# DeltaNet and SwiGLU on one core: where chunk 2 makes the sums of the gate and value weights

## The chip, the cores and the metric

The kernel runs on one NeuronCore of a Trainium2 chip, in float32 throughout. The metric is the time of one execution on the device in microseconds (us). A core has five engines that run side by side, each through its own instructions in order: TensorE (PE in the profile; PEld is its loading of weights), VectorE (DVE), ScalarE (ACT), GpSimd (POOL) and SyncE (SP), which here only issues DMA transfers. Where one engine needs another's result it waits on a semaphore.

## The reference

Four sequences with eight heads of size 48 go through a delta-rule attention over 768 steps. Its output, laid side by side by head (3072 tokens of 384 numbers), goes through a SwiGLU block with 1536 hidden units.

```python
k_n = k / (norm(k) + 1e-6)
for t in range(S):
    y[t]  = q[t] @ state
    v_old = k_n[t] @ state
    state = state + beta[t] * outer(k_n[t], v[t] - v_old)
x = y.transpose(0, 2, 1, 3).reshape(B * S, H * D)
g = x @ w_gate
out = (g * sigmoid(g) * (x @ w_val)) @ w_out
```

## The kernel before

**Chunks.** The 768 steps are cut into 12 chunks of 64. For a chunk, attention turns K and Q, makes products of K with K and of Q with K (`gram`), inverts a triangular matrix for each head and two chunks (`invert`, with `substitute` as 31 steps of two VectorE operations), joins the halves of that inverse (`join_1`, `join`), and carries the state forward in four steps (`advance`): first p_r and p_y, the products of K and Q with the state, and the subtraction of p_r from V (L770); then p_u (L775), copied into `uu`; then p_s and p_y (L806, L794); then the transposes p_f and the copy into `x_ffn` (L843). The FFN of chunk c, 256 tokens, runs on TensorE while attention of chunk c + 1 is threaded through it.

**The FFN of chunk 2.** `FAST` is 3. Chunks 0 to 2 compute the FFN plainly, chunks 3 to 11 by a scheme of block sums which saves products (`gate_val_fast`, `output_fast`) and which needs sums of blocks of the weights. Chunk 2 is the last plain one (`c == FAST - 1`). Its loop (L1443) runs over six pairs of hidden blocks, f = 0, 2, 4, 6, 8, 10. `gate_val` (L1002) does for each pair: the gate product (12 matmul instructions at L1009), SiLU on ScalarE (L1018), the value product (12 more), the product of the two on VectorE (L1023, called h here), then `point`, the sums, and `fill`. The outputs of the chunk's two halves follow (`output`, L1036, with a copy at L1044 and two stores issued by ScalarE at L1053).

**What threads attention in.** `point(c + 1)` issues one piece of the next chunk's attention. In the six pairs of chunk 2 these are, in order: the second half of a join (L639); the transposes of K and Q (L424), behind each of which stand eight block loads of the next chunk into the buffer just read, issued by SP (L169); the gram products (L447) with the masking of one result on VectorE (L465); then the first three steps of `advance`. `fill(n)` spends about n units on the inverse (the steps of `substitute`, L519 and L525, the transposes of `turn`, L489, those at L687 and L692, and four ScalarE copies at L698) and stops in the middle where n runs out; the next `fill` goes on from there. So the order on each engine is fixed by the order of these calls. No scheduler changes it.

**The sums.** `sums_of_w(f)` (L880) does two things. For three of the pairs it makes one set r of three sums, each in two VectorE operations of 128x256 (L1080, L1077), and stores each to device memory as soon as it is ready, by SP (L894). The three sums have one buffer each, used for all three sets: `w_s[1]` is h_f_99, `w_s[2]` is h_f_100, and `w_s[4]` is half of p_sb_125. So the next set can't be written until the last one's stores have landed. The set r = 0 stays in the buffers for the first round of chunk 3; the others are loaded back later (L941). For f of 6 and more it also overwrites two blocks of the weights with a difference (two operations, L1077), so the sums that need such a block must have been made by then. In the kernel before, the sets are made at pairs 2, 4 and 6, in the order r = 1, 2, 0.

**What follows.** After both outputs, `join` of the next inverse begins (L716 on TensorE, L722 on ScalarE), and chunk 3's first fast round (L917) starts: a product p_x, copied by ScalarE to p_y (L945), a product p_w, and a product that accumulates on p_y (both from L928).

Of the kernel before, what the change touches and what calls it, by code (L numbers as in the profile page):

```python
# [20 lines left out]
def kernel(  # L21
# [57 lines left out]
    def ps_ffn(shape, name, bank=None):  # L79
        if bank is None:  # L80
            taken.append(name)
            bank = (len(taken) - 1) % 4
        n = 1
        for m in shape[1:]:
            n *= m
        p = ffn_banks[bank][:, 0:n]
        return p if len(shape) == 2 else p.rearrange("p (x n) -> p x n", x=shape[1])
# [225 lines left out]
    for b in range(2):  # L313
# [5 lines left out]
            fill=0.0,  # L319
# [536 lines left out]
    def new_h(c, f, at):  # L856
        hs[c, f] = hp[at].rearrange("p (i n) -> p i n", i=2)
# [17 lines left out]
    def w_pair(m, t, f):  # L875
        return (wg_sb, wv_sb)[m][:, t, 128 * f : 128 * f + 256].rearrange(
            "p (i n) -> p i n", i=2
        )

    def sums_of_w(f):  # L880

        if 2 <= f <= 6:
            r = f // 2 % 3
            f1, f2 = 2 * r, 2 * r + 6
            for n in (1, 2, 4):
                for m in range(2):
                    s_ = w_s[n][:, 2 * m : 2 * m + 2]
                    if n == 1:
                        plus(s_, w_pair(m, 0, f2), w_pair(m, 1, f2))
                    elif n == 2:  # L890
                        minus(s_, w_s[1][:, 2 * m : 2 * m + 2], w_pair(m, 0, f1))
                    else:
                        minus(s_, w_pair(m, 1, f1), w_s[2][:, 2 * m : 2 * m + 2])
                nc.sync.dma_start(out=kept[n, r], in_=w_s[n])  # L894
        if f >= 6:
            for m in range(2):
                minus(w_pair(m, 0, f), w_pair(m, 0, f - 6), w_pair(m, 0, f))
# [104 lines left out]
    def gate_val(c, f, fill, within=None, behind=None):  # L1002

        ps = {}
        for w_sb, name in ((wg_sb, "p_gate"), (wv_sb, "p_val")):
            ps[name] = ps_ffn([128, 2, TOK], name)
            for i in range(2):
                for t in range(KT):
                    nc.tensor.matmul(  # L1009
                        ps[name][:, i],  # L1010
                        w_sb[:, t, (f + i) * 128 : (f + i + 1) * 128],
                        xts[c][:, t],
                        start=(t == 0 and (i == 0 or c < 2)),
                        stop=(t == KT - 1),
                        skip_group_check=True,
                    )
            if name == "p_gate":
                nc.scalar.activation(sil, ps[name], ACTF.Silu)  # L1018
                fill(2)
                if within is not None:  # L1020
                    point(within)
        new_h(c, f, len(hs) if c < 2 else f // 2)
        nc.vector.tensor_tensor(out=hs[c, f], in0=sil, in1=ps["p_val"], op=ALU.mult)  # L1023
        if behind is not None:
            point(behind)
        if c == FAST - 1:
            sums_of_w(f)
        fill(3)

    def output(c, bp, fill, between=()):  # L1030
        p_o = ps_ffn([128, DM], "p_o", bp if c == FAST - 1 else None)
# [28 lines left out]
    FAST = 3  # L1060
# [15 lines left out]
    def minus(out, a, b):  # L1076
        nc.vector.tensor_tensor(out=out, in0=a, in1=b, op=ALU.subtract)  # L1077

    def plus(out, a, b):
        nc.vector.tensor_tensor(out=out, in0=a, in1=b, op=ALU.add)  # L1080
# [92 lines left out]
    def converts(n):  # L1173
        if todo:
            convert(todo[:n])
            del todo[:n]
# [36 lines left out]
    def fill_some(n):  # L1213
        while n > 0 and fills:
            did = next(fills[0][1], 0)
            if did == 0:
                inverted.add(fills.pop(0)[0])
            if did == WAIT:
                return
            n -= did or 1  # L1220
# [51 lines left out]
    def point(c):  # L1272

        mine = c < NCH and steps("advance", c) < 4 and may_advance(c)
        if mine and steps("advance", c) > 0:
            step("advance", advance, c)
        elif not prep_step(c - 1) and mine:
            step("advance", advance, c)
# [12 lines left out]
    def fill(n):  # L1291
        if todo:

            filled.append(n)
            converts(2 if len(filled) < 4 else 1)
            if len(filled) == 1:
                converts(1)
        else:
            after_weights()
            fill_some(n)  # L1300
# [3 lines left out]
    def after_weights():  # L1304
        if not done:
            done.append(1)
            nc.gpsimd.memset(ztp[1], 0.0)
            fills.insert(0, (1, second_inverse[0]))
# [6 lines left out]
    with tc.manual_schedule(  # L1315
# [101 lines left out]
        for c, f in pairs:  # L1417
            early = c == 0 and f < 8
            if c == 1 and f == 0:
                finish(1)  # L1420
            elif f > 0:
                point(1 if early else 2)
            need((6, 12, 18, 18, 24, 24)[f // 2])
            gate_val(c, f, fill, 1 if early else None)
# [11 lines left out]
        for c in range(2, NCH):  # L1436
            point(c + 1)
            if c >= FAST:
                for r in range(ROUNDS):
                    gate_val_fast(c, r, fill)  # L1440
                output_fast(c, fill)
            else:
                for f in range(0, FT, 2):  # L1443
                    gate_val(c, f, fill, behind=c + 1)
                output(c, 0, fill)
                point(c + 1)
                output(c, 1, fill)
            finish(c + 1)
            x_sums(c + 1)
# [30 lines left out]
```

## Time and profile before

| | us |
|---|---|
| runs of the kernel before (four) | 725.7, 726.38, 724.74, 723.41 |
| median | 725.22 |
| the profiled execution | 725.7 |
| its span, first to last instruction | 724.0 |
| TensorE busy in the span | 685.5 |
| VectorE busy | 464.4 |
| ScalarE busy | 255.0 |
| the gate and value products of chunk 2 (L1009) | 190.09 to 235.4 |
| its two outputs (L1036) | 237.35 to 253.8 |
| first matmul of chunk 3's FFN (L928) | 254.91 |

Times inside the execution count from the first instruction. In a line of the timeline, the first number is the start, the second the time from the start of the first to the end of the last of the instructions merged into it, and in brackets stands how long the engine was idle before, and what ended that. A name like `h_f<-wg_sb` is output, arrow, input, buffer numbers left out. PEclk is the clock that TensorE was granted, as a share of full speed. A line that starts with SPq or ACTq is the issue of a transfer and not the transfer itself.

### The profile page before, as it was taken

How to read it: one execution, taken by the hardware profiler on the slowest of the kernel's cores; microseconds unless marked ns; L12 is line 12 of the kernel's file. 1: busy time of each engine (PE TensorE's matmuls, PEld its weight loads, DVE VectorE, ACT ScalarE, POOL GpSimd, SP SyncE). 2: the span in 40 equal slices, each digit the busy share in tenths (PEclk: the TensorE clock that was granted, in tenths of full speed). 3: DMA queues.
4: the chain of work that ended last, by engine and by line, in shares of the span. 5: the costliest groups of instructions: out<-in, count | busy, mean ns of one | idle time of the engine just before them, and what ended most of it. 6: DMA issues, size and time to landing. Idle time of an engine off the chain costs nothing.

```text
span 724.0 us, 25286 instructions
## 1 busy us (share of the span) xinstructions
PE 685.5 (95%) x11212; PEld 631.0 (87%) x11212; DVE 464.4 (64%) x1052; ACT 255.0 (35%) x536; POOL 51.8 (7%) x46
## 2 busy tenths in 40 slices
PE   4658999999998999999999999999999999999997
PEld 3546788866786699999999999999999999999997
DVE  5995765776379656688765889559864436233442
ACT  3567755302421243234334224323153033132230
POOL 7003000203000002100020000300000000000000
PEclk9656999999998999999999999999999999999999
DMA  6785454221144025255425434135143222131210
GB/s 146 177 242 147 124 116 126 43 35 24 36 66 133 13 65 115 58 110 118 60 69 110 69 75 99 50 75 107 53 95 95 40 73 68 26 86 45 67 44 23
DMA packets 143278, 60.19 MB, mean 83 GB/s; under 512 B 124256, under 2 KB 127328, under 8 KB 143168
## 3 DMA queue, kind: packets, MB, share of 16 engines
q1 hardware_dynamic: 139712, 56.82, 34.0%
q10 hardware_dynamic: 3072, 1.57, 1.0%
q8 instruction: 88, 1.44, 0.8%
q0 software_dynamic: 384, 0.17, 0.1%
q14 instruction: 22, 0.18, 0.1%
HBM read 51.46 MB, written 7.08 MB: 81 GB/s over the span
## 4 chain that ended last, share of the span: by engine, by line
PE 83%; DVE 5%; SPq 4%; DMA 3%; ACT 3%; issue 2%; ACTq 0%; DVEq 0%
PE ffn L928 36%; PE ffn L1123 16%; PE ffn L1009 11%; PE ffn L1036 6%; PE p_g L447 2%; PE p_u L775 2%; PE p_s L806 1%; PE p_r L753 1%; PE p_y L794 1%; PE p_y L762 1%; SPq L136 1%; SPq L250 1%; DMA vin<-in_v_dram 1%; DMA kn<-in_k_dram 1%; PE p_f L840 1%
## 5 line engine op out<-in xcount | busy, mean ns | idle before, releaser
L928 PE MATMUL ffn<-x_ffn,wg_sb 128*128 128x128 f32 x756 | 116.2, 276 | 0.3 <-DVE ffn L1080 0.3
L928 PE MATMUL ffn<-x_ffn,wv_sb 128*128 128x128 f32 x756 | 115.3, 275 | 0.0
L928 PEld LDWEIGHTS ffn<-x_ffn,wg_sb 128*128 128x128 f32 x756 | 99.6, 192 | 0.9 <-DVE ffn L1080 0.5
L928 PEld LDWEIGHTS ffn<-x_ffn,wv_sb 128*128 128x128 f32 x756 | 99.6, 192 | 0.0
L948 ACT ACTIVATE sil<-ffn 128x256 f32<-128x256 f32 x108 | 41.5, 385 | 122.5 <-PE ffn L928 120.5
L953 DVE TENSOR_TENSOR h_f<-sil,ffn 128x256 f32<-128x256 f32 x108 | 44.6, 418 | 48.8 <-ACT sil L948 46.8
L1123 PE MATMUL ffn<-wo_sb,h_f 128*128 128x192 f32 x432 | 75.2, 327 | 0.0
L1123 PEld LDWEIGHTS ffn<-wo_sb,h_f 128*128 128x128 f32 x432 | 70.3, 190 | 0.3
L1080 DVE TENSOR_TENSOR ffn<-ffn,p_sb 128x512 f32<-128x512 f32 x54 | 37.6, 697 | 49.9 <-ACT ffn L974 48.9
L525 DVE TENSOR_TENSOR zb<-zb,tmp 128x31 f32<-128x31 f32 (+15 forms) x186 | 63.7, 343 | 6.4
L519 DVE TENSOR_TENSOR tmp<-zb,mb 128x31 f32<-128x31 f32 (+15 forms) x186 | 63.3, 341 | 6.4 <-PE p_j L639 1.3
L1009 PE MATMUL ffn<-x_ffn,wg_sb 128*128 128x256 f32 x216 | 55.7, 412 | 1.6 <-ACT x_ffn L843 1.6
L928 PE MATMUL ffn<-x_t,h_f 128*128 128x128 f32 x432 | 54.3, 279 | 0.5 <-ACT ffn L945 0.5
L928 PEld LDWEIGHTS ffn<-x_t,h_f 128*128 128x128 f32 x432 | 50.9, 191 | 1.3 <-ACT ffn L945 0.7
L1009 PEld LDWEIGHTS ffn<-x_ffn,wg_sb 128*128 128x128 f32 x216 | 43.3, 206 | 8.8 <-ACT x_ffn L843 2.1
L661 POOL TENSOR_TENSOR n_b<-mb,half 128x32 f32<-128x32 f32 x5 | 28.0, 5595 | 308.1 <-DVE mb L489 268.6
L1009 PE MATMUL ffn<-x_ffn,wv_sb 128*128 128x256 f32 x216 | 49.9, 380 | 0.0
L1080 DVE TENSOR_TENSOR o_sb<-o_sb,ffn 128x192 f32<-128x192 f32 x45 | 15.8, 351 | 51.3 <-PE ffn L1123 44.3
L1036 PE MATMUL ffn<-wo_sb,h_f 128*128 128x384 f32 x136 | 45.7, 490 | 0.0
L1009 PEld LDWEIGHTS ffn<-x_ffn,wv_sb 128*128 128x128 f32 x216 | 40.7, 190 | 5.5
L1036 PEld LDWEIGHTS ffn<-wo_sb,h_f 128*128 128x128 f32 x136 | 25.3, 190 | 16.5
L945 ACT COPY ffn<-ffn 128x512 f32<-128x512 f32 x27 | 15.4, 570 | 56.6 <-PE ffn L928 47.9
(229 smaller groups left out, 1040.0 us busy)
## 6 DMA issues: line engine op xcount, KB each, us to landing
h_f<-w_s SPq DMA_DIRECT2D x52, 256.0 KB
p_sb<-w_s SPq DMA_DIRECT2D x26, 256.0 KB
vin<-in_v_dram SPq DMA_DIRECT2D x96, 48.0 KB
kn<-in_k_dram SPq DMA_DIRECT2D x40, 96.0 KB
out_dram<-o_sb SPq DMA_DIRECT2D x36, 96.0 KB
zt<-in_moe_w_out_dram SPq DMA_DIRECT2D x6, 384.0 KB
qpad<-in_q_dram SPq DMA_DIRECT2D x36, 64.0 KB
wo_sb<-in_moe_w_gate_dram SPq DMA_DIRECT2D x4, 512.0 KB
```

The source lines that it names most:

```text
L447: nc.tensor.matmul(p_v[par][half_of(b if of_q else b ^ par), bp, j], kt[c][half_of(par), bp, j, b], xt[half_of(par), bp, j, b],)
L519: nc.vector.tensor_tensor(out=t_v, in0=zb[:, 0 : j + 1, j : j + 1].to_broadcast([128, j + 1, m]), in1=mb[:, j : j + 1, j + 1 : R].to_broad ...
L525: nc.vector.tensor_tensor(out=zb[:, 0 : j + 1, j + 1 : R], in0=zb[:, 0 : j + 1, j + 1 : R], in1=t_v, op=ALU.add,)
L661: nc.gpsimd.tensor_tensor(out=n, in0=mb.rearrange("p j i -> p (j i)")[:, 0 : R * R : R + 1], in1=half, op=ALU.pow,)
L928: nc.tensor.matmul(p[:, u], w(u), moving, start=start and u == 0, stop=True, skip_group_check=True,)
L945: nc.scalar.copy(p_y, p_x)
L948: nc.scalar.activation(sil[:, n].rearrange("p (i n) -> p i n", i=2), p[:, 0:2], ACTF.Silu)
L953: nc.vector.tensor_tensor(out=h_of(c, f, j), in0=sil[:, n].rearrange("p (i n) -> p i n", i=2), in1=p[:, 2:4], op=ALU.mult,)
L1009: nc.tensor.matmul(ps[name][:, i], w_sb[:, t, (f + i) * 128 : (f + i + 1) * 128], xts[c][:, t], start=(t == 0 and (i == 0 or c < 2)), stop ...
L1036: nc.tensor.matmul(p_o, hs[c, f - f % 2][:, f % 2, bp * 128 : (bp + 1) * 128], wo_sb[:, f], start=(f == 0), stop=(f == FT - 1),)
L1080: nc.vector.tensor_tensor(out=out, in0=a, in1=b, op=ALU.add)
L1123: nc.tensor.matmul(p[x, part], a(f - f % 2)[:, f % 2], b(f), start=not begun and f == 0, stop=f == FH - 1, skip_group_check=True,)
```

## The change

The three sets are made at pairs 0, 2 and 4, still in the order r = 1, 2, 0. At pairs 2 and 4 they stand ahead of `point`, so ahead of the transposes of K and Q (pair 2) and of the masking (pair 4), on VectorE and, with their stores, on SP. At pair 0 they stand behind `point`, where the call was. The differences for f of 6 and more stay where they were. The `fill` at the end of pairs 0, 2, 4 and 6 is 2 units, not 3.

```diff
     def sums_of_w(f):
-        if 2 <= f <= 6:
-            r = f // 2 % 3
+        if f <= 4:
+            r = (f // 2 + 1) % 3
             f1, f2 = 2 * r, 2 * r + 6
...
         nc.vector.tensor_tensor(out=hs[c, f], in0=sil, in1=ps["p_val"], op=ALU.mult)
+        if c == FAST - 1 and 0 < f < 6:
+            sums_of_w(f)
         if behind is not None:
             point(behind)
-        if c == FAST - 1:
+        if c == FAST - 1 and not 0 < f < 6:
             sums_of_w(f)
-        fill(3)
+        fill(2 if c == FAST - 1 and f <= 6 else 3)
```

`fill` also stands inside `gate_val`, after SiLU, with 2 units; it is not changed. On VectorE and SP the order of the new kernel's instructions around the edit is: at pair 0, h, the six operations of set 1, then seven steps of `substitute`; at pair 2, h, set 2, the two transposes, five steps; at pair 4, h, set 0, the two maskings, four steps. On SP the stores of sets 1 and 2 come before the sixteen block loads, those of set 0 after them. On ScalarE, one copy of L698 stays before the copy into `x_ffn`, and three move behind the second output's copy and stores. TensorE's instructions and GpSimd's keep their order.

## The prediction

> **What bounds the kernel now.** I read the page first, for the engine that is nearly always busy and for the slices where it is not.
>
> ```profile
> PE 685.5 (95%) x11212; PEld 631.0 (87%) x11212; DVE 464.4 (64%) x1052; ACT 255.0 (35%) x536; POOL 51.8 (7%) x46
> ...
> PEclk9656999999998999999999999999999999999999
> ```
>
> TensorE (PE) is busy 95% of the span. Its clock is low in the first slices, which the change doesn't touch, and once more in the thirteenth (217 to 235 us), which is chunk 2, where the edit lies. So I asked for the waits between 184 and 256 us, from the end of chunk 1's output to the start of chunk 3 (us in total, times, longest).
>
> ```profile
> DVE h_f L1080 <- DMA w_s<-h_f: 3.6, 1, 3.6
> ...
> PE p_u L775 <- DVE vin L770: 2.9, 1, 2.9
> ```
>
> TensorE stands still for 2.9 us, for VectorE (DVE); VectorE stands still for 3.6 us, for a store. The timeline of that window (start, us, engine, instruction) joins the two:
>
> ```profile
> 208.96 5.08 SPq L169 DMA_DIRECT2D qpad<-in_q_dram  x8
> ...
> 214.13 2.02 SPq L894 DMA_DIRECT2D w_s<-h_f  x2
> ...
> 217.49 0.43 DVE L1080 TENSOR_TENSOR h_f<-wg_sb 128x256 f32<-128x256 f32 x1 [3.60 <-DMA w_s<-h_f]
> ...
> 225.75 1.96 PE L775 MATMUL p_u<-vin,zt 64*64 64x48 f32 x64 [2.94 <-DVE vin L770]
> ...
> 227.64 5.18 PE L1009 MATMUL ffn<-x_ffn,wg_sb 128*128 128x256 f32 x12
> ```
>
> The first sum of weights is ready at 206.5, but SyncE (SP) issues 16 block loads of K and Q from 204.8 to 214.0, and the store follows only at 214.13. The next sum overwrites the same buffer, so VectorE waits until 217.49, everything behind it is late, L770 too (224.75), which hands p_u its input, and TensorE, through with the value product of pair 8 at 222.8, starts p_u at 225.75. Twelve gate matmuls then take 5.18 us where the same row takes 2.86 at 217.37. The windows view shows why (length; PE, PEld, DVE, ACT, POOL busy; then the granted clock):
>
> ```profile
> 27.60:31.01 3.41, 1.92 (x130) 1.78 (x124) 3.17 (x8) 1.07 (x2) 0.00 (x0) 1.00 1.00 242
> 31.01:34.43 3.42, 1.40 (x82) 1.26 (x84) 3.15 (x9) 2.06 (x6) 0.00 (x0) 1.00 0.50 95
> 222.16:225.57 3.41, 0.66 (x4) 0.23 (x2) 3.27 (x7) 0.60 (x1) 0.00 (x0) 1.00 0.00 0
> 225.57:228.98 3.41, 3.23 (x67) 2.96 (x68) 3.38 (x11) 0.80 (x1) 0.00 (x0) 0.50 0.51 188
> ```
>
> After a window with TensorE busy for 0.66 of 3.41 us comes one at half clock (and a second, to 232.40, also at 0.50). The stall is thus paid twice.
>
> [...]windows of that length laid from 225.57 fit every change of clock; one busy 0.56 (27.60) kept the clock, one busy 0.41 (31.01) lost it. [...]here the first store frees its buffer 3.36 us after its issue (214.13 to 217.49), and I use that.
>
> **The change part by part.** Matmuls keep their number, their order and what they wait for; VectorE, ScalarE (ACT) and SP are reordered.
>
> *Pair 0* gets a set of six sums. They take 1.98 us (205.84 to 207.82), after h at 196.25. VectorE has an idle 1.28 us here, waiting for the join's matmuls (L639) until 197.60; the sum into p_sb, whose old content those matmuls read, can start no earlier, so four sums fit in the wait and two (0.67 us) come after it. One substitution step of 0.77 us less follows (fill of 2, not 3). VectorE reaches pair 2 at 202.5, where h waits for its matmuls until 202.95 as before. Cost nothing. The stores go out from 196.96 on an SP that is idle from 188.6 to 204.8.
>
> *Pair 2:* sums from 203.56 to 205.54, now ahead of the transposes of K and Q. Their buffer must be free: issue 196.96 + 3.36 = 200.3, so 3.2 us to spare. The transposes end at 206.7 and 207.8 instead of 204.8 and 205.9; their products on TensorE start at 207.95 and 208.94, so 1.1 us or more to spare. Five substitution steps (0.77+0.81+0.84+0.87+0.77) bring h of pair 4 to 211.9, before 212.01. On SP the three stores go from 204.2, and the 16 loads start about 2 us later, at 206.7; they are for the next chunk. Cost nothing.
>
> *Pair 4:* the third set from 212.5 to 214.5; its buffers' stores left at 204.2 to 205.6, landed at about 209. The masking of p_g (L465, 1.28 us at 212.61) moves behind the sums and ends at 215.75. L762, which overwrites that PSUM, starts at 216.32: 0.6 us to spare, the tightest place. Four steps (3.5 us) bring h of pair 6 to 219.3 (before 224.16), and L770 ends at 220.9 (before 225.7). The gain on VectorE, 4.8 us, is the wait of 3.6, plus one step and the overlaps of its neighbours. TensorE finishes the value product of pair 8 at 222.8, so p_u starts without a wait, 1.9 us in hand.
>
> *The gain.* The stall of 2.94 us goes. Without it the clock stays full: p_u and 24 gate and value matmuls cost 1.96 + 7.70 = 9.66 us in the chain of waits; at full clock 1.08 (p_u at 181.42) + 5.39 (24 matmuls at 197.47) = 6.47. That is 3.19. Together 6.13 us. Next late would be h of pair 10, needed by the output product some 6.7 us after 231.2; VectorE has it at about 232.4.
>
> *Pairs 6 to 10 and the price.* Fewer steps per fill let the substitution end later in the list. Of the four ScalarE copies L698, which stood together before x_ffn's copy, three now stand behind the second output's copy and its two DMA issues, before L722 and L945 (ScalarE's timeline):
>
> ```profile
> 247.07 2.28 ACT L698 COPY zt<-zt 32x512 f32<-32x512 f32 x4 [1.20 <-DVE vin L403]
> ...
> 253.80 0.48 ACT L1044 COPY o_sb<-ffn 128x384 f32<-128x384 f32 x1 [3.62 <-PE ffn L1036]
> 254.31 1.12 ACTq L1053 DMA_DIRECT2D out_dram<-o_sb  x2
> 255.48 0.60 ACT L722 ACTIVATE t<-p_j 128x512 f32<-128x512 f32 x1 [1.20 <-PE p_j L716]
> 256.10 0.57 ACT L945 COPY ffn<-ffn 128x512 f32<-128x512 f32 x1
> ```
>
> TensorE runs 16 matmuls L928 in 1.98 us from 255.90; the second eight (from 256.79) accumulate on what L945 writes; L945 ended at 256.67, so there is 0.1 us of cover. Three copies at a pitch of 0.56 put L945 1.67 us later: TensorE stalls 1.6 us. The ends are 0, if part of it is hidden by something I don't see, and 1.6 + 3.2 = 4.8, if the stall halves the clock as before: wholly inside one window it leaves it 0.53 busy, between the 0.41 that lost the clock and the 0.56 that kept it, and about half the time the window's edge splits it. I take 1.6.
>
> **Sum.** 725.7 (the profiled execution, span 724.0) − 6.13 + 1.6 = 721.2. The median of the four runs is 725.22; from there it would be 720.7. I say 721.0.
>
> **Rivals.** *Clock lost at the new stall* (half clock for one or two windows): 722.6 to 724.2. For it: 0.53 is close to the edge. Against: split windows are busier. *The copies cost nothing:* 719.3. Against: the cover is 0.1 us. *No gain*, 725: another VectorE delay eats the 1.9 us before p_u, or L762 waits for the mask; the 0.6 us at L762 speak for it, every other spare time against. *Slower:* the stores of pair 0 land late. VectorE would wait at 203.56 with the transposes, the masks and all else behind it. A landing of 6.6 us is free; w us beyond that stall TensorE by w − 0.6 at L762[...]. Against it: 3.36, 2.49 and 2.79 us are what the stores take in this trace, amid block loads, and between 195 and 205 us the DMA engines are 1% busy. That the stores don't go ahead is excluded: SP's instruction order has two sets of stores before the loads.
>
> **How the numbers follow.** Forecast 0.64, around 721.0 (719.8 to 722.4); clock lost 0.14; copies free 0.09; no gain 0.06; slower 0.07. A measurement here tells from no change what is over 0.3%, 2.2 us. Faster: 0.64 + 0.09 + 0.04 of the lost clock (one window only) = 0.77; same 0.10 + 0.06 = 0.16; slower 0.07. The range runs from 719.0 to 724.2 and leaves out no gain, slower, and a little at its edges.
>
> **What would show it.** Right: no wait of L775 for L770, no wait of VectorE for a store in chunk 2, clock 1.00 through 217 to 240 us, p_s (L806) near 229.2 instead of 235.34, and a wait of L928 for ACT L945 of 1.6 us at about 251. Wrong: L762 waiting for L465, a wait of L1080 for a store near 203.6, a clock of 0.5 near 252, or L945 on time.

## The result and the profile after

| | us |
|---|---|
| before, median of 64 runs | 723.76 (719.95 to 726.79) |
| changed, median of 43 runs | 721.02 (719.69 to 723.16) |
| ratio of changed to before | 0.9966, 95% interval 0.9957 to 0.9975 |
| profiled execution before, span | 725.7, 724.0 |
| profiled execution changed, span | 719.06, 717.3 |

The change makes the kernel faster by 0.34% (0.25 to 0.43%), which is 2.5 us (1.8 to 3.1). The two profiled executions lie further apart, 6.6 us. Chunk 2 began 2.1 us earlier in the second one (first gate matmul at 187.95, not 190.09), the edited stage took 6.1 us less, and what follows it took 1.6 us more, most of it the price at L945 (below). The profile before happened to be an expensive execution, as is shown below.

The lines from 1024 on are numbered two higher in the changed kernel (L1077 became L1079, L1080 became L1082, L1036 became L1038, L1044 became L1046). Its waits of TensorE between 180 and 262 us (us in total, times, longest):

```profile
PE ffn L928 <- ACT ffn L945: 1.4, 1, 1.4
PE ffn L1009 <- ACT x_ffn L843: 0.9, 1, 0.9
```

The wait of p_u for L770 is gone, and the wait that the prediction had priced at 1.6 us is there with 1.44 in this view. The second line is old: before the change it stood at 0.7. The timeline of the same stretch shows the room at each step:

```profile
202.20 0.99 SPq L894 DMA_DIRECT2D w_s<-h_f  x2
203.54 0.32 SPq L894 DMA_DIRECT2D w_s<-p_sb  x1
204.70 4.79 SPq L169 DMA_DIRECT2D qpad<-in_k_dram  x8
...
212.37 1.28 DVE L465 TENSOR_TENSOR p_sb<-p_g,mask_q 128x512 f32<-128x512 f32 x2
...
214.19 1.11 PE L762 MATMUL p_y<-state,qt 64*64 64x48 f32 x64
...
217.68 0.95 DVE L770 TENSOR_TENSOR vin<-vin,p_r 128x768 f32<-128x768 f32 x1
...
220.61 1.15 PE L775 MATMUL p_u<-vin,zt 64*64 64x48 f32 x64
221.69 2.86 PE L1009 MATMUL ffn<-x_ffn,wg_sb 128*128 128x256 f32 x12
```

The stores of the second set stand ahead of the block loads. The masking ends 0.5 us before L762 overwrites what it read, and L770 ends 2.0 us before p_u starts. The gate product behind p_u takes 2.86 us again, not 5.18. The windows view of the changed kernel has the clock at full speed from 217 to 240 us (columns as before):

```profile
217.00:240.00 23.00, 23.00 (x272) 17.11 (x271) 20.82 (x51) 5.10 (x9) 0.00 (x0) 1.00 0.18 43
```

And ScalarE's timeline after the second output has the price:

```profile
245.52 0.48 ACT L1046 COPY o_sb<-ffn 128x384 f32<-128x384 f32 x1 [5.42 <-PE ffn L1038]
246.03 1.12 ACTq L1055 DMA_DIRECT2D out_dram<-o_sb  x2
247.19 1.76 ACT L698 COPY zt<-zt 32x512 f32<-32x512 f32 x3 [1.20 <-issue]
248.98 0.60 ACT L722 ACTIVATE t<-p_j 128x512 f32<-128x512 f32 x1
249.47 0.59 ACT L945 COPY ffn<-ffn 128x512 f32<-128x512 f32 x1
```

The three copies stand between the output's stores and L722. Without them L722 could have started at about 247.2, right behind the stores' issue, as it did in the kernel before; L945, which TensorE needs, is late by that. TensorE's timeline:

```profile
246.63 0.71 PE L928 MATMUL ffn<-x_ffn,wg_sb 128*128 128x128 f32 x4
...
250.12 1.16 PE L928 MATMUL ffn<-x_t,h_f 128*128 128x128 f32 x8 [1.44 <-ACT ffn L945]
251.12 0.61 PE L928 MATMUL ffn<-x_ffn,wg_sb 128*128 128x128 f32 x4
```

The 1.44 us count from the end of the matmul before, which the profile only models. Counted from start to start the delay is longer: the last row starts 4.49 us after the first, in the kernel before 2.81 us after it (254.91 to 257.72). So the price is 1.68 us.

### The profile page after: what moved, and what is told of

Read it like the earlier page. It is cut to its first block, busy times and chain, and to the rows that moved or that the text cites. A ratio compares the mean times of both kernels' runs of the same rounds, so it can differ in the third digit from the quotient of the medians.

```text
span 717.3 us, 25292 instructions
## 1 busy us (share of the span) xinstructions
PE 682.5 (95%) x11212; PEld 629.5 (88%) x11212; DVE 464.0 (65%) x1052; ACT 254.8 (36%) x536; POOL 51.8 (7%) x46
## 3 DMA queue, kind: packets, MB, share of 16 engines
q8 instruction: 88, 1.44, 0.9%
## 4 chain that ended last, share of the span: by engine, by line
PE 85%; DVE 4%; SPq 4%; ACT 3%; DMA 2%; issue 1%; ACTq 0%; DVEq 0%
PE ffn L928 36%; PE ffn L1125 16%; PE ffn L1009 12%; PE ffn L1038 6%; PE p_g L447 2%; PE p_u L775 2%; PE p_r L753 2%; PE p_s L806 2%; PE p_y L794 1%; PE p_y L762 1%; SPq L250 1%; PE p_f L840 1%; SPq L136 1%; DMA kn<-in_k_dram 1%; DMA vin<-in_v_dram 1%
## 5 line engine op out<-in xcount | busy, mean ns | idle before, releaser
L928 PE MATMUL ffn<-x_ffn,wg_sb 128*128 128x128 f32 x756 | 116.2, 276 | 0.3 <-DVE ffn L1082 0.3
L928 PE MATMUL ffn<-x_ffn,wv_sb 128*128 128x128 f32 x756 | 115.3, 275 | 0.0
L928 PEld LDWEIGHTS ffn<-x_ffn,wg_sb 128*128 128x128 f32 x756 | 99.6, 192 | 0.9 <-DVE ffn L1082 0.5
L928 PEld LDWEIGHTS ffn<-x_ffn,wv_sb 128*128 128x128 f32 x756 | 99.6, 192 | 0.0
L1082 DVE TENSOR_TENSOR ffn<-ffn,p_sb 128x512 f32<-128x512 f32 x54 | 37.6, 697 | 53.4 <-ACT ffn L974 52.4
L928 PE MATMUL ffn<-x_t,h_f 128*128 128x128 f32 x432 | 54.6, 279 | 2.0 <-ACT ffn L945 2.0
L1009 PE MATMUL ffn<-x_ffn,wg_sb 128*128 128x256 f32 x216 | 52.1, 392 | 1.9 <-ACT x_ffn L843 1.9
L928 PEld LDWEIGHTS ffn<-x_t,h_f 128*128 128x128 f32 x432 | 50.9, 191 | 2.9 <-ACT ffn L945 2.3
L1082 DVE TENSOR_TENSOR o_sb<-o_sb,ffn 128x192 f32<-128x192 f32 x45 | 15.8, 351 | 51.4 <-PE ffn L1125 48.4
L1009 PEld LDWEIGHTS ffn<-x_ffn,wg_sb 128*128 128x128 f32 x216 | 41.0, 195 | 8.2 <-ACT x_ffn L843 2.4
L1038 PE MATMUL ffn<-wo_sb,h_f 128*128 128x384 f32 x136 | 45.7, 490 | 0.0
L1009 PEld LDWEIGHTS ffn<-x_ffn,wv_sb 128*128 128x128 f32 x216 | 40.7, 190 | 5.5
L1038 PEld LDWEIGHTS ffn<-wo_sb,h_f 128*128 128x128 f32 x136 | 25.3, 190 | 16.5
L945 ACT COPY ffn<-ffn 128x512 f32<-128x512 f32 x27 | 15.4, 571 | 56.6 <-PE ffn L928 47.9
```

The lines of the kernel that those rows point to most:

```text
L928: nc.tensor.matmul(p[:, u], w(u), moving, start=start and u == 0, stop=True, skip_group_check=True,)
L945: nc.scalar.copy(p_y, p_x)
L1009: nc.tensor.matmul(ps[name][:, i], w_sb[:, t, (f + i) * 128 : (f + i + 1) * 128], xts[c][:, t], start=(t == 0 and (i == 0 or c < 2)), stop ...
L1038: nc.tensor.matmul(p_o, hs[c, f - f % 2][:, f % 2, bp * 128 : (bp + 1) * 128], wo_sb[:, f], start=(f == 0), stop=(f == FT - 1),)
```

## The experiments

Runs of one kernel vary by some us among themselves (the 64 of the kernel before by 6.8), so two measures are used. One is the median of many runs. The other is a distance inside one trace, from the first gate matmul of chunk 2 to the first matmul of p_s. It holds the whole edited stage, doesn't depend on when chunk 2 began, and repeats to the last digit shown (39.12) in the five traces without a stall or a loss of clock in it.

| kernel | first gate matmul to p_s, us | wait for L945, us | median, us | ratio to before, 95% interval |
|---|---|---|---|---|
| before, first profile | 45.25 | 0 | 723.76 (this run 725.7) | |
| before, e9 | 41.86 | 0 | 721.91 (one run) | |
| before, e10 | 45.18 | 0 | 725.74 (one run) | |
| changed | 39.12 | 1.44 | 721.02 | 0.9966 (0.9957 to 0.9975) |
| changed, again (e8) | 39.12 | 1.44 | 720.94 | 0.9968 (0.9957 to 0.9979) |
| e1, stores ahead only | 40.80 | 0 | 719.28 | 0.9935 (0.9913 to 0.9957) |
| e2, pairs moved only | 42.93 | 1.44 | 723.61 | 1.0007 (0.9991 to 1.0022) |
| e3, copies early | 39.12 | 0 | 719.07 | 0.9935 (0.9914 to 0.9955) |
| e4, stall filled | 42.45 | 0 | 722.23 | 0.9983 (0.9971 to 0.9996) |
| e5, copies doubled | 39.12 | 3.37 | 724.14 | 1.0011 (0.9997 to 1.0025) |
| e6, fills only | 42.83 | 1.44 | 724.86 | 1.0004 (0.9987 to 1.0022) |
| e7, fills kept | 39.12 | 0 | 719.29 | 0.9937 (0.9917 to 0.9957) |

From p_s on to chunk 3's first FFN matmul all of them take 19.56 to 19.57 us. The kernel before, run beside e1 to e4, had a median of 723.2; beside e5 to e8, 723.37.

The theory was the prediction's: the stores' place on SyncE frees VectorE, the stall at p_u costs its length and then the clock, and the late copies cost the wait at L945. The rivals: the move to pair 0 or the short fills make the room, the half clock has no part, or the copies are hidden.

**Parts of the change, one at a time.** The change has three: sums and stores ahead of the transposes and loads, sets at earlier pairs, shorter fills.

e1 has the first part alone (to the kernel before):

```diff
+        if c == FAST - 1 and f < 6:
+            sums_of_w(f)
         if behind is not None:
             point(behind)
-        if c == FAST - 1:
+        if c == FAST - 1 and f >= 6:
             sums_of_w(f)
```

> The kernel before with one thing changed: at pairs 2 and 4 the sums and their stores stand ahead of the transposes and block loads. Pairs stay 2, 4, 6, fills stay 3. Theory (the stores' place on SyncE is what frees VectorE): no VectorE wait for a store, p_u (L775) starts without a stall, clock 1.00 from 217 to 240 us, and since the four copies L698 stay in front of x_ffn's copy, no stall at L945 either; p_s about 6 us earlier than in the kernel before when counted from the first gate matmul of chunk 2, and 1 to 2 us faster than the changed kernel. Rival (the move of the first set to pair 0 is what makes room on VectorE): p_u still waits for L770 by 1 us or more, and the time is between before and after.

From the first gate matmul to 262 us TensorE waits for no other engine, and VectorE waits for no store. The start of p_u and the clock from 217 to 240 us (columns as before):

```profile
224.41 1.15 PE L775 MATMUL p_u<-vin,zt 64*64 64x48 f32 x64
```

```profile
217.00:240.00 23.00, 23.00 (x391) 18.18 (x391) 21.87 (x56) 3.42 (x6) 0.00 (x0) 1.00 0.36 96
```

The median is 1.7 us below that of e8 (measured on another chip, where the kernel before differs by 0.2 us). So the move to pair 0 isn't what frees VectorE. One thing was not expected: the distance is 40.80, not 39.12, because the first gate product itself ran at half clock.

```profile
187.18:190.59 3.41, 2.38 (x73) 1.88 (x73) 2.05 (x5) 1.93 (x4) 0.24 (x1) 1.00 0.46 104
190.59:194.00 3.41, 3.41 (x9) 2.69 (x8) 0.00 (x0) 1.07 (x3) 0.00 (x0) 0.50 0.01 2
```

One stretch of 3.41 us at half clock, which costs 1.68 us (40.80 − 39.12). It comes ahead of anything the edit touches, and e10 has the same at the same place (190.73 to 194.14). Because of it p_s came 4.45 us earlier than in the first profile and not the expected 6.

e2 has the pairs and the fills of the changed kernel, but the sums behind `point` again (to the changed kernel):

```diff
-        if c == FAST - 1 and 0 < f < 6:
-            sums_of_w(f)
         if behind is not None:
             point(behind)
-        if c == FAST - 1 and not 0 < f < 6:
+        if c == FAST - 1:
             sums_of_w(f)
```

> The changed kernel with all sums behind the transposes again: pairs 0, 2, 4 and fills of 2, but the stores of the second set stand behind the sixteen block loads. Theory: the wait for a store comes back one set later, at pair 4, by about 3 us (the stores leave SyncE at about 214 us on the clock of the kernel before), p_u waits for L770 by 1 to 2.5 us, and the stall at L945 by 1.4 us is there as well, because the fills are short: no faster than the kernel before, 723 to 726. Rival (moving the sets to earlier pairs is enough): no stall at p_u, time as the changed kernel.

The timeline of e2:

```profile
215.00 1.67 SPq L894 DMA_DIRECT2D w_s<-h_f  x2
...
218.04 0.42 DVE L1080 TENSOR_TENSOR h_f<-wg_sb 128x256 f32<-128x256 f32 x1 [3.83 <-DMA w_s<-h_f]
...
225.33 1.15 PE L775 MATMUL p_u<-vin,zt 64*64 64x48 f32 x64 [2.08 <-DVE vin L770]
226.41 4.52 PE L1009 MATMUL ffn<-x_ffn,wg_sb 128*128 128x256 f32 x12
```

As the theory had it: the wait for the store is back with 3.83 us, one set later, p_u waits 2.08, and 1.66 us more go to the clock (4.52 us for a gate product, not 2.86). No gain. The rival falls.

e6 has the short fills alone (to the kernel before):

```diff
-        fill(3)
+        fill(2 if c == FAST - 1 and f <= 6 else 3)
```

> The kernel before with the short fills alone (2 units at pairs 0 to 6), sums and stores where they were. Theory: one substitution step fewer behind the wait for the store brings h of pair 6 forward by about 1 us, so p_u waits 2 us instead of 2.9, and the late copies bring the stall of 1.4 us at L945: 0.5 us slower than the kernel before but for the clock, 722.5 to 724.5. Rival (the short fills are what frees VectorE ahead of p_u): no stall at p_u, faster by 2 us or more.

The wait of p_u shrinks to 2.02 us, the wait for L945 appears with 1.44 (us in total, times, longest):

```profile
PE p_u L775 <- DVE vin L770: 2.0, 1, 2.0
PE ffn L928 <- ACT ffn L945: 1.4, 1, 1.4
```

The median of 724.86 is 0.4 us above the range expected, and the ratio can't be told from 1. The fills don't free VectorE to any purpose.

e7 is the changed kernel with all fills left at 3, and e3 the changed kernel with a longer fill behind the first output, which brings the copies forward in another way:

```diff
-        fill(2 if c == FAST - 1 and f <= 6 else 3)
+        fill(3)
```

```diff
-        fill(4 if c < 2 else 7)
+        fill(4 if c < 2 else 8.5 if c == FAST - 1 and bp == 0 else 7)
```

> The changed kernel with the fills left at 3 units. Theory: VectorE runs 0.3 us late at pair 2 and 1.3 us late at pair 6, inside the room of 0.5 at L762 and 1.9 at p_u, no stall there, and all four copies L698 come early: 1.4 us faster or more than the changed kernel, 719 to 719.6. Rival (the fills had to be cut for the sums to fit): p_u waits for L770 or L762 for the masking, and the time is 720 or above.

> The changed kernel with one number changed: the fill behind the first output of chunk 2 is 8.5 units, not 7, so that all four copies L698 stand in front of x_ffn's copy. Theory: the stall of 1.4 us of L928 for L945 goes, nothing else moves, 1.4 us faster than the changed kernel, or more if that stall costs the clock in some executions (then up to 2.5). Rival (the 1.4 us is hidden or taken up again by a later wait): same time as the changed kernel.

In both the wait for L945 is gone and the distance is 39.12, so VectorE had room for the longer fills: in e7 L770 ends at 220.67 and p_u starts at 221.37. ScalarE's timeline of e7:

```profile
239.55 2.28 ACT L698 COPY zt<-zt 32x512 f32<-32x512 f32 x4 [1.20 <-DVE vin L403]
```

e7 is 1.65 us below e8 in the median (719.29 against 720.94, same chip), and the slowest of its six runs (719.73) is below the fastest of the 22 of e8 (719.92). That is the whole price: from the first row of L928 to the row behind the stall e8 takes 4.48 us, e7 2.81. e3, on another chip, has 719.07. The short fills brought nothing and cost this much.

e8 is the changed kernel itself, as the measure for e5 to e7:

> The changed kernel once more, beside the others on the same chip: 720.5 to 721.5, with the stall of 1.4 us at L945. It is the measure for the others.

It repeats: 720.94.

**The clock.** e4 leaves the stall at p_u in the kernel before and keeps TensorE busy in it: the gate product of pair 10 is computed once more than needed, ahead of p_u.

```diff
+        if c == FAST - 1 and f == 8:
+            again = ffn_banks[len(taken) % 4].rearrange("p (i n) -> p i n", i=2)
+            for i in range(2):
+                for t in range(KT):
+                    nc.tensor.matmul(
+                        again[:, i],
+                        wg_sb[:, t, (10 + i) * 128 : (11 + i) * 128],
+                        xts[c][:, t],
+                        start=(t == 0 and i == 0),
...
         if behind is not None:
             point(behind)
```

> The kernel before with the stall of 2.9 us at p_u filled: the gate product of pair 10 (12 matmul instructions, 2.7 us) is computed once more ahead of p_u, into the bank where it is computed again afterwards. The stall is not shortened, only made busy. Theory (the stall costs twice, its length and then the clock): clock 1.00 from 217 to 240 us and, with the stall's length still there, faster than the kernel before by 3.2 us where that lost the clock for two windows, by nothing where it did not lose it; 1 to 3 us in the median. Rival (the half clock has another cause, or costs nothing): same time as the kernel before, or slower by up to 0.5 us.

Its p_u and its clock from 217 to 240 us:

```profile
226.50 1.15 PE L775 MATMUL p_u<-vin,zt 64*64 64x48 f32 x64 [0.67 <-DVE vin L770]
```

```profile
217.00:240.00 23.00, 22.33 (x328) 18.00 (x321) 20.50 (x56) 3.42 (x6) 0.00 (x0) 1.00 0.40 123
```

Twelve matmul instructions more, and the kernel is faster: 722.23 against 723.2, ratio 0.9983, at the lower end of what was expected. Its 22 runs lie within 2.7 us of each other (721.35 to 724.0), the 43 of the kernel before within 6.1 (720.26 to 726.32): its slow ones are gone, its fastest ones too. The clock of its trace is 1.00 from 217 to 240 us. The store's wait in that trace is 4.1 us and the distance 0.6 longer than that of e9 (42.45 − 41.86), so what the clock cost the kernel before in the median can be estimated as 1.0 + 0.6 = 1.6 us. The 0.6 comes from one trace of each.

e5 goes the other way. It makes a stall of that length elsewhere: the three late copies are made twice in the changed kernel.

```diff
                 nc.scalar.copy(z[:, :, 0:R], z[:, :, R:C])
+                if g == 2 and (s, c) != (0, 0):
+                    nc.scalar.copy(z[:, :, 0:R], z[:, :, R:C])
```

> The changed kernel with the three late copies L698 made twice (the second time with the same values), so that L945 is late by three copies more, 1.7 us at their pitch of 0.56. Theory (a stall of TensorE of about 3 us costs its length and, in part of the executions, the clock): L928 waits for L945 by 3.1 us, and the median is 1.7 plus 1 to 2 us above the changed kernel, 723.5 to 725; executions spread wider than those of the changed kernel. Rival (the clock has no part in it): 1.7 us above the changed kernel, 722.7, with the same spread.

TensorE's timeline of e5 (its lines are two higher again):

```profile
253.00 1.67 PE L930 MATMUL ffn<-x_t,h_f 128*128 128x128 f32 x8 [3.37 <-ACT ffn L947]
254.46 1.06 PE L930 MATMUL ffn<-x_ffn,wg_sb 128*128 128x128 f32 x4
```

The same four matmuls take 0.61 us in the changed kernel, where the clock is 1.00 from 240 to 257 us; in e5 it is 0.51 from 253.51 to 256.92. The stall grew by 1.93 us (3.37 − 1.44), the median by 3.2 (724.14 − 720.94), so about 1.3 us is clock by this estimate, and the runs spread over 3.3 us (722.74 to 726.03) against 2.8 of e8. The rival's 722.7 is the fastest run of the fourteen.

e9 and e10 are two more executions of the unchanged kernel. They ask whether that loss is the same each time:

> The kernel before, unchanged, looked at once more. Theory[...]: the stall of p_u is 2.9 us again within 0.5, but the stretch at half clock behind it differs from look to look: none, one window or two. Rival (the loss is the same in every execution): 6.8 us at half clock again.

> As the look before it: a stall of p_u of 2.4 to 3.4 us, and a stretch at half clock of 0, about 3.4 or about 6.8 us. The rival expects 6.8.

The wait of p_u is 2.67 us in both. In e9 the clock changes at 66.72 us and at 718.67, 191 times 3.4133 us apart (in the first profile 68.54 and 225.56 are 46 times that apart). Stretches of this length, laid on from one change, are the windows here; that their borders count also where the clock doesn't change is a reading that was not shown. In e9, 46 windows after 66.72, a border falls at 223.73, inside the stall (221.98 to 224.65). The windows on both sides of that border in e9, then in e10 the one that holds nearly the whole stall and the next:

```profile
220.32:223.73 3.41, 1.66 (x8) 1.13 (x6) 3.20 (x9) 0.00 (x0) 0.00 (x0) 1.00 0.07 28
223.73:227.14 3.41, 2.49 (x71) 2.28 (x72) 3.41 (x9) 1.40 (x2) 0.00 (x0) 1.00 0.30 112
```

```profile
224.87:228.28 3.41, 0.99 (x64) 0.99 (x64) 3.34 (x8) 0.60 (x1) 0.00 (x0) 1.00 0.00 0
228.28:231.69 3.41, 3.41 (x20) 2.70 (x13) 3.27 (x10) 0.80 (x1) 0.00 (x0) 0.50 0.71 246
```

e9 loses no clock in the edited stage, e10 one window of 3.41 us behind the stall, the first profile two (6.83 us). In e9 the border splits the stall into 1.75 and 0.92 us, and TensorE is busy for 0.49 and 0.73 of the two windows. In e10 it is busy for 0.29 of the one, in the first profile for 0.19. So the same stall of 2.67 us cost clock in e10, where it lay nearly whole in one window, and none in e9, where a border split it; that is one trace of each. The rival, the same loss in every execution, falls. Why the first profile lost a second window isn't shown: the window behind its stall was busy for 3.23 of 3.41 us and that of e10 throughout, but whether the missing 0.18 us decided that was not tried.

## Why the prediction was right, and what was mis-sized

- *What bounds the kernel, and the wait for the store.* Right. e1 and e2 show that the stores' place ahead of the sixteen loads decides, and with it alone the stall goes.
- *Pair 0 costs nothing.* Right: from h to the first substitution step VectorE takes 2.62 us (193.50 to 196.12) where it took 1.96 with the wait (195.64 to 197.60), so 0.66 us more, forecast 0.67; h of pair 2 still waited 0.47 for its matmuls.
- *Pairs 2 and 4.* Right: 0.5 us to spare at L762 (forecast 0.6), 2.0 at p_u (1.9). h of pair 10 came earlier than said, 40.7 us after the first gate matmul, where the prediction's 232.4 would be 42.3; nothing hung on it.
- *The gain in the profiled execution.* Right: 45.25 − 39.12 = 6.13 us, the number forecast.
- *The price at L945.* Right in kind and in size: the row behind the stall comes 1.68 us later, forecast 1.6 (1.44 in the view of waits). e3 and e7 show it by itself.
- *The sum.* Here a term was mis-sized. The 3.19 us of the clock were read from one execution, which had lost two windows, and were taken over to the median as they stood. The three traces of the kernel before show 0, about 1.6 and about 3.1 us of clock (41.86; 43.5 without the loss at e10's first gate product; 45.25, of which 0.27 over e9 is a longer wait), and e4 puts the median's share at about 1.6. With that, 2.74 (41.86 − 39.12) + 1.6 − 1.68 = 2.7 us; measured 2.74 between the medians and 2.5 by the ratio.
- *The base.* The four runs known beforehand had a median of 725.22, 64 runs have 723.76. In the sum that starts from the profiled execution (721.2), base and clock term were too high together, so the end holds. The sum from the median (720.7) took the loss of two windows off a median that, by the estimate above, holds about half of it. That 721.0, a number between the two, met 721.02 so closely is luck. The gain forecast from the median, 4.2 us, was 1.5 us too large.
- *The rivals.* Clock lost at the new stall shows in none of the four traces with that stall (the changed kernel, e8, e2, e6): four matmuls L928 behind it take 0.61 us in each. In e2 the stall (255.06 to 256.51) lies whole in one window (253.70 to 257.11), the case that the prediction put at 0.53 busy and near the edge; TensorE is busy there for 1.97 of 3.41 us (0.58), and the clock stays full. Free copies are excluded by e3 and e7. Late stores (the slower side) didn't occur; no wait of VectorE for a store is left.

What stays open: the fastest run of the kernel before (719.95) comes within 0.3 us of the fastest of the changed one (719.69), while the shortest distance seen before is 2.74 us longer and the price of L945 gives back only 1.68 of it. The start of chunk 2 by itself differs by 2.6 us among the traces (187.95 to 190.52), which is more than the 0.8 us that are left, but none of the three traces of the kernel before shows such a run.

Faster than the changed kernel are e7, e3 and e1, which can't be told apart (719.29, 719.07, 719.28): the changed kernel without its short fills, with one longer one, or the kernel before with only the call of the sums moved at pairs 2 and 4. e1 is the smallest edit, and has about 0.65% where the change has 0.34%.

## What to carry to other kernels

Where an engine waits for a small transfer, look at what stands ahead of it on the queue that issues it: here sixteen loads that nobody needed soon took 9 us to issue, and the store that freed a buffer stood behind them. The stall of TensorE had two terms here: its length, which nearly repeats (2.94, 2.67 and 2.67 us), and the clock after it, which was at half for 6.83, 0 and 3.41 us in the same three traces. So the second is taken as a mean over executions and not from the one profile. And when work is threaded in by a budget, a smaller budget moves the rest to a later place: ask which engine's queue that place is in, and who waits behind it.

## What the runs showed of the hardware

The changes of the clock lie whole multiples of 3.4133 us apart, in the changed kernel (191 between 64.77 and 716.71 us) and in e10 (11 between 190.73 and 228.28) as in the first profile and e9 above. The borders laid from them fall at another place of the kernel each time: the first one behind the first gate matmul of chunk 2 comes 1.34 us after it in the first profile, 3.11 in the changed kernel, 0.35 in e9 and 0.52 in e10.

Laid out so, the windows that hold the stall of p_u, or in e5 that of L945, sort by TensorE's busy share: with 0.14 (e5), 0.19 (first profile), 0.29 (e10), 0.39 (e2) and about 0.41 (e6) half clock followed; with 0.49 and 0.73 (e9), and at the wait for L945 of 1.44 us with 0.58 (e2) and 0.70 (the changed kernel), the clock stayed full. That wait cost the clock in none of its four traces (the changed kernel, e8, e2, e6); the stalls of 2.02 us and more (e6 2.02, e2 2.08, e10 2.67, the first profile 2.94, e5 3.37) cost it in all but e9 (2.67).

The busy share doesn't decide by itself. In e1 a window with 2.38 of 3.41 us busy (0.70, 187.18 to 190.59) was followed by half clock, and in e10 one with 2.37; in the changed kernel one with 2.38 (249.09 to 252.50) was followed by full clock. The windows of e1 and e10 hold six matmuls of the transposes p_f and 64 of 32x32 of a join (L629); whether these matter was not tried.
